# The convolutions' second stage on sixteen 32x32 tiles of TensorE, with another order of channels and the engines' order tied by hand

## The chip, the cores and the metric

The kernel runs on one core of a Trainium2 chip. The metric is the device time of one execution in microseconds (us). The engines are named as in the profile: PE (TensorE's matmuls; PEld its weight loads), DVE (VectorE), ACT (ScalarE), POOL (GpSimd) and SP (SyncE, which here only issues DMAs). PE writes to PSUM, which has eight banks, and reads SBUF.

## What is computed

Four residual layers over x of 2048 rows by 640 channels: attention, convolution, attention, convolution, each behind a layer norm.

```python
x = x + _A_ref(_layernorm(x), A_wqkv, A_wo)      # 32 heads of 20, softmax
x = x + _B_ref(_layernorm(x), ...)
x = x + _A_ref(_layernorm(x), A_wqkv, A_wo)
x = x + _B_ref(_layernorm(x), ...)

def _B_ref(u, log_A_real, A_imag, C_real, C_imag, log_dt, D_skip):
    ...
    K = 2.0 * jnp.einsum("dn,dnl->dl", C, P).real        # a kernel of 2048 taps a channel
    Kf = jnp.fft.rfft(K, L2)                              # L2 = 2 * 2048
    Uf = jnp.fft.rfft(u_t, L2)
    y = jnp.fft.irfft(Uf * Kf[None, :, :], L2)[:, :, :L]
    ...
    return y + u * D_skip[None, None, :]
```

Both convolutions use the same K, so it is made and transformed once.

## The kernel before, in words

Position l of the 2048 is 16 p + i, with p on the 128 partitions and i from 0 to 15. The transforms are written as matmuls in two stages: a first over p (matrix `e1`, 128 frequencies k), a second over i (matrix `f2`, 16 by 16, real and imaginary parts), then the product with the transformed K, and the two stages back (`fa` over i, `eb` over p). Channels go in five blocks of 128 (`NCT`).

**Convolution** (`ssm`). A block has eight steps, 40 in all, n in the code, and some more at the end for the pipeline. Step n of the loop issues:
- `stage2a(n)`: eight f16 transposes of what the first stage left in x1 (the high and the low half of each value), 4 groups of channels, to PSUM `pst`; ACT copies it to `xt`.
- `stage2b(n-1)`: three matmuls of 128 rows by 512 columns with `f2` into `psx`. `f2` is 16 by 16 repeated for the four channels of a group (128 rows: 32 of i and part, 4 channels). Then the product: DVE shuffles psx (real and imaginary parts change places) to t2 and multiplies psx by ka to t1; POOL multiplies t2 by kb and adds the two. ka and kb are loaded from the DRAM tensors `kha`, `khb`.
- `stage1` of the next block: twelve matmuls to PSUM psx1, ACT casts it to x1's high half, DVE subtracts for the low half.
- `stage3(n-3)`: `fa` on the product t1, to `psv`; ACT copies it to v.
- in every second step from n = 11 `stage4`: sixteen rows of records (eight f32 matmuls in two passes) with `eb` to `psy`; DVE adds psy to x, and in the first convolution takes the statistics for the next layer norm (`bn_stats`, four).

In the last block's steps (n from 32) there is no first stage. The last four `stage4` follow the loop. PSUM has the pools X, M, T and F of two banks each: psx1 in X, pst in T, psx in F, psv and psy in M.

**The transform of K** (`ktransform`) does the same two stages with f32 values and no way back: transposes of K by time, first stage, transposes of x1 (`kx`), and one f32 matmul with `f2` for each four groups; DVE writes its result out twice with `stream_shuffle` (real parts doubled, imaginary parts doubled), ACT puts the sign on one, and both go to `kha` and `khb`. It is a generator whose pieces are issued inside the **output projection** of the first attention (`out_proj`, 16 rows s of 30 matmuls `po`). The framework orders instructions by what is ready; where an order is wanted, `tie` makes one instruction follow another on its engine.

The first attention makes K itself (`kgen`) between its exponentials, with an order that a plan sets; `bound` there works out a scale, `ksc`, that the transform uses. `prefetch` loads what the projection needs while the attention ends.

Of the kernel before, what the change touches and what calls it, by code (L numbers as in the profile page):

```python
# [21 lines left out]
P = 128  # L22
# [65 lines left out]
def mha_s4d_kernel(ctx, tc, x_in, wqkv, wo, lar, aim, cr, ci, ldt, dsk,  # L88
                   c_e1, c_eb, c_f2, c_fa, c_sel, c_lv, c_id, c_sg, c_e16, c_f16, c_id16, c_dn, out, parts="asas", general=None):
# [28 lines left out]
    kha = dram.tile([P, D // 4, P], F32, name="kha")  # L118
    khb = dram.tile([P, D // 4, P], F32, name="khb")
# [69 lines left out]
    def chain(ins):  # L189
        last[0] = tie(ins, last[0])  # L190

    def kgen():
# [166 lines left out]
        for n, t in enumerate((ld["cr"], ld["ci"], skip)):  # L359
            ve.reduce_max(big[:, n:n + 1], t, axis=AX.X, apply_absolute_value=True)  # L360
# [12 lines left out]
        slow.append((1, bound))  # L373
        load_powers(2)
        yield
# [771 lines left out]
    def prefetch(x, rest):  # L1147
# [16 lines left out]
        if rest:  # L1164
            with tc.tile_pool(name="wos", bufs=NCT, side="right") as ws:
                for ct in range(NCT):
                    wt = ws.tile([P, D], F32, name="wot")
                    sy.dma_start(wt, wo[ct * P:ct * P + P, :])
                    ge.tensor_copy(woh[:, ct, :], wt)
                    ge.tensor_sub(wol[:, ct, :], wt, woh[:, ct, :])  # L1170
# [20 lines left out]
    ups = []  # L1191
# [16 lines left out]
    SWAP = list(range(16, 32)) + list(range(16))  # L1208
    DUP0 = list(range(16)) * 2
    DUP1 = list(range(16, 32)) * 2  # L1210

    def by_channel(x1, i2):
        return x1[:, :, i2].rearrange("p g (s c) -> p s g c", c=4)

    def ktransform(e1):

        c = ExitStack()
        c1 = c.enter_context(tc.tile_pool(name="f1", bufs=1))
        c2 = c.enter_context(tc.tile_pool(name="f2", bufs=2))
        f2 = c1.tile([P, P], F32, name="f2")  # L1220
        sy.dma_start(f2, c_f2)
        sgn = c1.tile([P, 1], F32, name="sgn")
        sy.dma_start(sgn, c_sg)

        skip = c1.tile([P, NCT], F32, name="skip")
        sy.dma_start(skip, dsk)

        def load(b):
            kl = c2.tile([P, L], F32, name="kl")
            sy.dma_start(kl, kd[b * P:b * P + P, :])  # L1230
            return kl
        kls = [load(0)]

        def unit_load(b):
            kl = kls.pop()
            if b + 1 < NCT:
                kls.append(load(b + 1))
            ve.tensor_add(kl[:, 0:1], kl[:, 0:1], skip[:, b:b + 1])
            hi, lo = (c1.tile([P, NI, P], F16, name=f"ktr{n}") for n in "hl")
            klv = kl.rearrange("d (p i) -> d i p", i=NI)  # L1240
            for i4 in range(4):
                pt = pst("T", [P, 4, P], F32, tag="T", name="pkt")
                for i in range(4):
                    te.transpose(pt[:, i, :], klv[:, 4 * i4 + i, :], ident)
# [3 lines left out]
                yield  # L1248
            x1 = c1.tile([P, 32, NI // 2, 16], F32, name="kx1")
            for i2 in range(NI // 2):  # L1250
                ps = pst("X", [P, 2, 2, P], F32, tag="X", name="pkx")
                for i in range(2):
                    s = 2 * i2 + i
                    for r in range(2):
                        for n, (e, m) in enumerate(((0, hi), (0, lo), (1, hi))):
                            te.matmul(ps[:, r, i, :], e1[:, e, s, r, :], m[:, s, :], start=(n == 0), stop=(n == 2))
                (ve.tensor_copy if i2 % 4 == 1 else se.copy)(by_channel(x1, i2), ps.rearrange("p r i (g c) -> p (r i) g c", c=4))
                yield
            prev = None
            for q in range(9):  # L1260
                if q < 8:
                    pt = pst("T", [P, 4, P], F32, tag="T", name="pkt")
                    for g in range(4):
                        te.transpose(pt[:, g, :], x1[:, 4 * q + g].rearrange("p i s -> p (i s)"), ident)
                    xt = c2.tile([P, 512], F32, name="kxt")
                    se.activation(xt, pt.rearrange("p g k -> p (g k)"), AF.Copy, scale=ksc[:, 1:2])
# [436 lines left out]
```

## Time and profile before

| | us |
|---|---|
| three runs | 2677.0 to 2681.95, median 2681.47 |
| the profiled execution | 2680.85 |
| its span, first to last instruction | 2679.1 |

The mean granted clock of PE was 0.996 over the span. The stages of the profiled execution, in us from the start of the span:

| stage | from | to | length |
|---|---|---|---|
| first attention, with the making of K | 0 | 1102.9 | 1102.9 |
| its output projection, with the transform of K from 1133.5 to 1247.6 | 1102.9 | 1273.6 | 170.7 |
| last layer norms, first stage of the first block | 1273.6 | 1284.85 | 11.25 |
| first convolution | 1284.85 | 1425.1 | 140.25 |
| second attention | 1425.1 | 2470 | 1044.9 |
| its output projection, norms, first stage | 2470 | 2533 | 63 |
| second convolution | 2533 | 2672.5 | 139.5 |

The rows that the prediction quotes are of four kinds. A view by stretches has for each the length and the busy time and number of instructions of PE, PEld, DVE, ACT and POOL, then the granted clock and the DMA engines' share and rate. A view by order of time has start, length, engine, line, operation, what it writes and reads, shape and number of merged instructions, and in brackets the idle time of the engine before it and what ended it. The chain of waits is the work that ended last, followed back. Groups by line have the busy time, the mean in ns and the idle time before them. A busy PE row holds the tail of a matmul that overlaps the next; the pace is read from start to start. Line 78 is a helper through which DVE, ACT and the DMAs are called.

### The profile page before, as it was taken

Reading aid. Unit: us, or ns where it says so; the run is one execution under the profiler, and the core shown is the slowest. Engines: PE = TensorE matmul, PEld = TensorE weight load, DVE = VectorE, ACT = ScalarE, POOL = GpSimd, SP = SyncE. Lnnn points to the kernel's source line nnn. Section 1 sums busy time; section 2 is a strip of 40 time slices with the busy share of each in tenths; the row PEclk is TensorE's granted clock in tenths of the full one; section 3 lists DMA queues with packets and bytes.
Section 4 is the critical chain, followed back from the end, with each engine's and each line's share of the span. In section 5 each row is a group of like instructions: output and inputs, shape, how many; then the busy total and the mean of one; then the engine's idle time right before and its main releaser. Section 6 shows DMA issues by size and latency. Waiting matters only on the chain.

```text
span 2679.1 us, 116332 instructions
## 1 busy us (share of the span) xinstructions
PE 2530.0 (94%) x51106; PEld 1425.0 (53%) x51106; DVE 1516.0 (57%) x3451; ACT 2368.7 (88%) x2793; POOL 827.7 (31%) x1256
## 2 busy tenths in 40 slices
PE   7899999999999998899998999999999998999898
PEld 3445444444444443678896444454444443444788
DVE  8687777886855994477776333232233221154865
ACT  7889999999999999676655799999999999999564
POOL 1123323333323334301672122222222222222376
PEclk9999999999999999999999999999999999999999
DMA  6513222322221224364542121121121113222465
GB/s 210 181 49 86 67 76 55 87 55 76 52 61 49 54 68 155 110 233 162 189 151 69 40 59 50 50 58 47 45 65 38 54 30 93 69 67 60 145 190 162
DMA packets 186580, 242.18 MB, mean 90 GB/s; under 512 B 43376, under 2 KB 128976, under 8 KB 184400
## 3 DMA queue, kind: packets, MB, share of 16 engines
q1 hardware_dynamic: 150048, 188.35, 21.8%
q0 software_dynamic: 36016, 46.30, 7.0%
q8 instruction: 403, 6.60, 1.0%
q14 instruction: 113, 0.93, 0.1%
HBM read 158.50 MB, written 76.01 MB: 88 GB/s over the span
## 4 chain that ended last, share of the span: by engine, by line
ACT 52%; PE 25%; issue 10%; DVE 6%; DMA 3%; POOL 1%; SPq 0%; ACTq 0%; DVEq 0%; POOLq 0%
ACT pt L78 50%; PE pa L892 4%; PE psv L1419 3%; PE psy L1429 3%; PE S L858 3%; PE psx L1407 2%; PE m L611 1%; PE psx L1384 1%; PE po L1312 1%; DMA kop<-ks 1%; PE pst L1394 1%; PE pkf L1272 1%; DVE ktab L78 1%; PE po L1307 1%; PE pq L764 1%
## 5 line engine op out<-in xcount | busy, mean ns | idle before, releaser
L78 ACT ACTIVATE pt<-S 128x1024 f32<-128x1024 f32 x2048 | 1928.6, 1032 | 41.4 <-PE S L858 29.2
L892 PE MATMUL pa<-pt,V 64*32 64x512 f32 x16384 | 1100.9, 590 | 1.4 <-DVE oc L78 1.2
L858 PE MATMUL S<-qop,kop 61*32 61x512 f16 x16384 | 882.9, 381 | 85.2 <-ACT pt L78 68.4
L858 PEld LDWEIGHTS <-kop 61*32 61x32 f16 x16384 | 366.7, 89 | 741.1 <-issue 622.4
L892 PEld LDWEIGHTS pa<-pt,V 64*32 64x32 f32 x16384 | 315.1, 106 | 74.6 <-issue 9.7
L78 POOL DMA_DIRECT2D dn<-oc x252 | 124.5, 501 | 670.6 <-DVE oc L78 643.8
L78 DVE TENSOR_SCALAR qc<-m 128x512 f32<-128x512 f32 (+1 forms) x68 | 46.8, 689 | 303.6 <-PE m L611 303.6
L78 POOL DMA_DIRECT2D db<-dn x252 | 128.0, 514 | 135.1 <-DMA dn<-dr 132.1
L78 DVE COPY oc<-pa 128x512 f32<-128x512 f32 x64 | 44.1, 690 | 199.6 <-PE pa L892 191.9
L611 PE MATMUL m<-xh,wh 64*32 64x512 f16 x2560 | 147.9, 379 | 5.5 <-DVE qc L78 5.5
L78 POOL DMA_DIRECT2D ot<-oc x256 | 130.4, 516 | 71.6 <-DVE oc L78 42.8
L611 PE MATMUL m<-xh,wl 64*32 64x512 f16 x2560 | 148.1, 377 | 0.0
L611 PE MATMUL m<-xl,wh 64*32 64x512 f16 x2560 | 146.7, 376 | 0.0
L611 PEld LDWEIGHTS <-wh 64*32 64x32 f16 x5120 | 92.9, 93 | 78.4 <-issue 36.4
L78 ACT COPY xt<-pst 128x1024 f16<-128x1024 f16 x80 | 81.6, 1022 | 47.2 <-PE pst L1394 47.0
L1412 POOL TENSOR_TENSOR t<-t,kb 128x512 f32<-128x512 f32 x80 | 102.0, 1276 | 67.6 <-DVE t L78 66.7
L78 POOL DMA_DIRECT2D dn<-dr x63 | 35.3, 560 | 248.8 <-DVE dr L78 236.4
L78 DVE TENSOR_SCALAR V<-m 128x160 f32<-128x160 f32 x64 | 20.7, 324 | 158.5 <-PE m L577 158.5
L78 DVE TENSOR_TENSOR kb<-ktab 128x512 f32<-128x512 f32 x160 | 107.7, 692 | 0.0
L577 PEld LDWEIGHTS <-xh 128*128 128x128 f16 x960 | 79.7, 98 | 47.0 <-issue 31.6
L1413 POOL TENSOR_TENSOR t<-t,t 128x512 f32<-128x512 f32 x78 | 99.3, 1273 | 8.5 <-DVE t L78 2.6
L329 PEld LDWEIGHTS m<-kb,ka 128*32 128x32 f32 x3840 | 61.0, 109 | 72.1 <-issue 55.3
(305 smaller groups left out, 4020.7 us busy)
## 6 DMA issues: line engine op xcount, KB each, us to landing
ka<-kha SPq DMA_DIRECT2D x80, 256.0 KB
kb<-khb SPq DMA_DIRECT2D x80, 256.0 KB
db<-dn POOLq DMA_DIRECT2D x252, 64.0 KB, 2.6
kop<-ks SPq DMA_DIRECT2D x176, 80.0 KB
kpw<-wd POOLq DMA_DIRECT2D x60, 192.0 KB, 4.7
qop<-qs SPq DMA_DIRECT2D x256, 40.0 KB
ot<-oc POOLq DMA_DIRECT2D x256, 40.0 KB, 3.0
kha<-kn SPq DMA_DIRECT2D x20, 512.0 KB
```

The costliest lines, as they stand in the source:

```text
L78: made = f(out, *a, **k)
L329: chain(te.matmul(ps[32 * j:32 * j + 32, c8, :], a[n][:, ch, :], b[n][:, dd, :], start=(n == 0), stop=(n == 2), tile_position=(0, 32 * j)))
L577: chain(te.matmul(ps[:, :n], a_[:, ct, sl], m[:, ct, :], start=(k == 0), stop=(k == 14)))
L611: chain(te.matmul(ps[r][32 * t:32 * t + 32, :], a_[rows, ct, 32 * u:32 * u + 32], m[rows, ct, 512 * v:512 * v + 512], start=(k == 0), stop ...
L764: te.matmul(pq, a_[:, ct, :], m[:, ct, sl], start=(n == 0), stop=(n == 14))
L858: chain(te.matmul(S[32 * t:32 * t + 32, 512 * r:512 * r + 512], kt_[rows, kc + 32 * t:kc + 32 * t + 32], qt[rows, :], start=True, stop=Tru ...
L892: chain(te.matmul(pa[r][32 * j:32 * j + 32, :], V[rows, kt, VP * h:VP * h + 32], pts[j // 2][rows, 512 * (j % 2):512 * (j % 2) + 512], sta ...
L1407: te.matmul(px, f2[:, f, :], xt[:, k, :], start=(n == 0), stop=(n == 2))
L1412: ge.tensor_mul(t2, t2, kb)
L1413: (ge if g0 else ve).tensor_add(t1, t1, t2)
L1419: te.matmul(pv[:, g].rearrange("p r i c -> p (r i c)"), t1[:, g * P:g * P + P], fa, start=True, stop=True)
L1429: te.matmul(py[:, i, :], eb[:, 4 * i4 + i, r, :], v[:, r, 4 * i4 + i].rearrange("p g c -> p (g c)"), start=(r == 0), stop=(r == 1))
```

## The change

Channels of a block are grouped 32 apart (c, c+32, c+64, c+96) instead of four neighbours. After the transposes each of the four sits on 32 partitions of its own. The second stage then needs a 32 by 32 matrix for each channel, and four steps are done at once by `sets`: on each of the sixteen tiles of 32 by 32 three matmuls of 512 columns, into four PSUM banks. The transposes read x1 at a distance of 32 elements. The pool T goes; F has four banks for the four channels, and transposes and first stage share X. In the convolutions every engine's order is tied as issued.

```diff
@@ ssm @@
+            def at(name, made):
+                order[name] = tie(made, order.get(name))
...
-            def stage2a(x1, q):
-                pt = pst("T", [P, 2, 4, P], F16, tag="T", name="pst")
+            def stage2a(x1, q, xt):
+                pt = pst("X", [P, 2, 4, P], F16, tag="X", name="pst")
                 for k in range(2):
                     for g in range(4):
-                        te.transpose(pt[:, k, g, :], x1[k][:, 4 * q + g].rearrange("p i s -> p (i s)"), id16)
-                xt = c2.tile([P, 2, 512], F16, name="xt")
-                se.copy(xt, pt.rearrange("p k g c -> p k (g c)"))
-                return xt
+                        at("pe", te.transpose(pt[:, k, g, :], of_group(x1[k], 4 * q + g), id16))
+                at("act", se.copy(xt[:, :, q % 4], pt))
...
-                px = pst("F", [P, 512], F32, tag="F", name="psx")
-                for n, (f, k) in enumerate(((0, 0), (0, 1), (1, 0))):
-                    te.matmul(px, f2[:, f, :], xt[:, k, :], start=(n == 0), stop=(n == 2))
+            def sets(xt):
+                px = [pst("F", [P, 512], F32, tag=f"F{ch}", name=f"psx{ch}") for ch in range(4)]
+                for n, (f, k) in enumerate(((0, 0), (0, 1), (1, 0))):
+                    for ch in range(4):
+                        rows = slice(32 * ch, 32 * ch + 32)
+                        for g in range(4):
+                            mm(px[ch][32 * g:32 * g + 32, :].rearrange("p (q k) -> p q k", k=P), f2[rows, f, :],
+                               xt[rows, k, :, g, :], start=(n == 0), stop=(n == 2), tile_position=(32 * ch, 32 * g))
+                return px
...
+            def product(px, ka, kb, alone):
                 t2 = c2.tile([P, 512], F32, name="t2")
-                ve.stream_shuffle(t2, px, SWAP)
-                ve.tensor_mul(t1, px, ka)
-                ge.tensor_mul(t2, t2, kb)
-                (ge if g0 else ve).tensor_add(t1, t1, t2)
-                return t1
+                at("dve", ve.stream_shuffle(t2, px, SWAP))
+                at("dve", ve.tensor_mul(ka, px, ka))
+                for f, *a in (("tensor_mul", kb, t2, kb), ("tensor_add", ka, ka, kb)):
+                    if alone:
+                        at("dve", getattr(ve, f)(*a))
+                    else:
+                        at("pool", getattr(ge, f)(*a))
+                return ka
...
-            for n in range(NQ + 3 + 4):
+            for n in range(NQ + 9):
                 b, q = divmod(n, 8)
+                if n % 4 == 0 and 4 <= n <= NQ:
+                    px = sets(xt)
                 if n < NQ:
...
-                    xts[n] = stage2a(x1, q)
-                if 1 <= n <= NQ:
-                    t1s[n - 1] = stage2b((n - 1) // 8, (n - 1) % 8, xts.pop(n - 1))
+                    stage2a(x1, q, xt)
+                if 2 <= n < NQ + 2:
+                    ks[n - 2] = factors(*divmod(n - 2, 4))
+                if 4 <= n < NQ + 4:
+                    t1s[n - 4] = product(px[n % 4], *ks.pop(n - 4), n > NQ and n % 2 == 1)
...
-                if 3 <= n < NQ + 3:
+                if 5 <= n < NQ + 5:
...
-                    stage3(vs[bb], qq, t1s.pop(n - 3))
-                if 11 <= n < NQ + 3 and (n - 11) % 2 == 0:
+                    stage3(vs[m // 2], m % 2, ch, t1s.pop(n - 5))
+                if 13 <= n < NQ + 5 and n % 2:
...
@@ ktransform: one group on sixteen tiles, evacuated without shuffles @@
-                    px = pst("F", [P, 512], F32, tag="F", name="pkf")
-                    te.matmul(px, f2, prev, start=True, stop=True)
-                    for s in range(2):
-                        ve.stream_shuffle(kn[s][:, (q - 1) % 2, :], px, [DUP0, DUP1][s])
-                    se.activation(kn[1][:, (q - 1) % 2, :], kn[1][:, (q - 1) % 2, :], AF.Copy, scale=sgn)
+            def ends(t, xt, s, dst):
+                px = [pst("F", [P, 512], F32, tag=f"F{ch}", name=f"pkf{ch}") for ch in range(4)]
+                for ch in range(4):
+                    rows = slice(32 * ch, 32 * ch + 32)
+                    for g in range(4):
+                        matmul(px[ch][32 * g:32 * g + 32, :].rearrange("p (q k) -> p q k", k=P), f2[rows, s, :],
+                               xt[rows, :, g, :], start=True, stop=True, tile_position=(32 * ch, 32 * g))
...
+            steps = [(turned, 0, xts[0], 0), (turned, 0, xts[0], 1), (by_time, b + 1, 0), (ends, 0, xts[0], 0, kha),
+                     (turned, 1, xts[1], 0), (ends, 0, xts[0], 1, khb), (turned, 1, xts[1], 1), (by_time, b + 1, 1),
+                     (ends, 1, xts[1], 0, kha), (first_stage, b + 1, 0), (ends, 1, xts[1], 1, khb),
+                     (first_stage, b + 1, 1), (first_stage, b + 1, 2), (first_stage, b + 1, 3)]
...
@@ out_proj: each matmul of the first projection tied, a step of the transform after every six @@
+            matmul(*a, **k)
+            many[0] += 1
+            if many[0] % 6 == 0:
+                weave(1)
...
-                if s == 2:
-                    weave(1000)
...
@@ kgen @@
-        slow.append((1, bound))
         load_powers(2)
+        slow.append((3, bound))
...
@@ prefetch: the transform's tiles, with K's first block loaded while the attention ends @@
+            rest.extend((small, lambda: load_kl(0)))
...
@@ seq @@
-                psum(c, M=2, T=2, F=2)
+                psum(c, M=2, F=1)
```

`by_time`, `first_stage` and `turned` are the old pieces of the transform, each with two PSUM tiles of X. The sign and the doubling of the transform's results are now in its matrix `c_f2` (one for kha, one for khb). The products of steps 41 and 43 run on DVE alone.

What stands on the engines in the first convolution's loop. DVE, before, from the product t1_29529 to the addition of psy_29667, which is the psy behind that product's psv (psv_29660):

```order
L78 TENSOR_TENSOR t1_29529<-psx_29525,ka_29521 128x512
L78 TENSOR_TENSOR x11_29176<-psx1_29535,x10_29175 128x4x32x4
L78 TENSOR_TENSOR x_25341<-x_25341,psy_29557 128x4x128
L78 BN_STATS st5_28671<-x_25341 128x6 x4
L78 STREAM_SHUFFLE t2_29591<-psx_29586 128x512
L78 TENSOR_TENSOR t1_29590<-psx_29586,ka_29582 128x512
L78 TENSOR_TENSOR x11_29597<-psx1_29598,x10_29596 128x4x32x4
L78 STREAM_SHUFFLE t2_29640<-psx_29635 128x512
L78 TENSOR_TENSOR t1_29639<-psx_29635,ka_29631 128x512
L78 TENSOR_TENSOR x11_29597<-psx1_29645,x10_29596 128x4x32x4
L78 TENSOR_TENSOR x_25341<-x_25341,psy_29667 128x4x128
```

DVE, after, from the addition of one psy to that of the next, psy_30189, behind the psv of the product ka_29967:

```order
L78 TENSOR_TENSOR x_25341<-x_25341,psy_30039 128x4x128
L78 BN_STATS st5_28884<-x_25341 128x6 x4
L78 STREAM_SHUFFLE t2_30120<-psx0_30053 128x512
L78 TENSOR_TENSOR ka_29967<-psx0_30053,ka_29967 128x512
L78 TENSOR_TENSOR x11_29879<-psx1_30125,x10_29878 128x4x4x32
L78 STREAM_SHUFFLE t2_30161<-psx1_30054 128x512
L78 TENSOR_TENSOR ka_30008<-psx1_30054,ka_30008 128x512
L78 TENSOR_TENSOR x11_29879<-psx1_30166,x10_29878 128x4x4x32
L78 TENSOR_TENSOR x_25341<-x_25341,psy_30189 128x4x128
```

The kinds of rows follow each other as before; the product that an odd step's psv takes stood ahead of the previous psy's addition and now stands behind it.

PE, before, at the end of an odd step and the start of the next:

```order
L1384 MATMUL psx1_29645<-uh_26463,e1s_26468 128x128
L1419 MATMUL psv_29660<-fa_26471,t1_29529 128x128 x4
L1429 MATMUL psy_29667<-v_28954,eb_28682 128x128 x8
L1394 LDWEIGHTS x10_29175
L1394 MATMUL pst_29681<-id16_26470,x10_29175 128x128
```

PE, after, the same place ahead of the first rows of a set (48 matmuls of 32 partitions by 512 columns, psx0 to psx3):

```order
L1411 MATMUL psx1_30263<-uh_26471,e1s_26476 128x128
L1411 MATMUL psv_30278<-fa_26479,ka_30116 128x128 x4
L1411 MATMUL psy_30285<-v_29688,eb_28895 128x128 x8
L1411 LDWEIGHTS f2s_26477
L1411 MATMUL psx0_30299<-xt_30105,f2s_26477 32x512
L1411 LDWEIGHTS f2s_26477
L1411 MATMUL psx0_30299<-xt_30105,f2s_26477 32x512
```

psy stands directly behind psv in both; the set comes after psy, once in four steps, in place of three matmuls in each step.

PE at the start of the first output projection, before:

```order
L1307 MATMUL po<-woh,ol 128x320 x10
L1312 MATMUL po<-woh,oh 128x320
L1312 MATMUL po<-wol,oh 128x320
L1312 MATMUL po<-woh,oh 128x320
L1312 MATMUL po<-wol,oh 128x320
```

and after:

```order
L193 MATMUL po<-woh,ol 128x320 x6
L196 MATMUL pkt<-ident,kl 128x128 x8
L193 MATMUL po<-woh,ol 128x320 x4
L193 MATMUL po<-woh,oh 128x320
L193 MATMUL po<-wol,oh 128x320
L196 MATMUL pkt<-ident,kl 128x128 x8
```

The transform's transposes (pkt from kl) now stand among the first row's po, six apart, where before the first row's po stood together.

214 lines of the change are left out of this document (116 added, 98 removed).

## The prediction

> **What bounds the kernel now.** I read the chain of waits first, then the busy time of each engine by stage, then the order of time inside one stage. The chain's shares by engine:
>
> ```profile
> ACT 52%; PE 25%; issue 10%; DVE 6%; DMA 3%; POOL 1%; SPq 0%; ACTq 0%; DVEq 0%; POOLq 0%
> ```
>
> ACT's half is the exponentials of the two attentions, which the change leaves alone. Its stages are the first output projection with the kernels' transform inside it, and the two convolutions. In the view by stretches these are the first three rows (projection alone, with the transform, alone again) and the last two:
>
> ```profile
> 1102.90:1133.50 30.60, 28.44 (x191) 27.09 (x185) 21.96 (x56) 11.78 (x17) 15.68 (x22) 1.00 0.49 152
> 1133.50:1247.60 114.10, 112.90 (x925) 86.59 (x926) 86.65 (x236) 88.70 (x145) 5.64 (x4) 1.00 0.56 213
> 1247.60:1273.60 26.00, 26.00 (x173) 25.04 (x171) 19.57 (x56) 12.71 (x20) 8.26 (x6) 1.00 0.28 100
> ...
> 1284.85:1425.10 140.25, 137.82 (x1434) 123.03 (x1434) 101.88 (x260) 81.66 (x151) 104.79 (x93) 1.00 0.48 155
> ...
> 2533.00:2672.50 139.50, 136.98 (x1407) 121.49 (x1407) 84.90 (x169) 80.38 (x148) 100.02 (x79) 1.00 0.60 188
> ```
>
> PE (first number after the length) is busy nearly throughout all five; POOL comes to 105 of 140 us in a convolution. By shares PE binds and work taken from PE is time won. Whether that holds depends on latency, so here is one pair of steps of the first convolution in order of time (start, length, engine):
>
> ```profile
> 1336.04 1.95 PE L1429 MATMUL psy<-v,eb 128*128 128x128 f32 x16
> ...
> 1337.82 0.61 PE L1394 MATMUL pst<-id,x 128*128 128x128 f16 x8
> 1338.02 0.69 DVE L78 TENSOR_TENSOR x<-x,psy 128x512 f32<-128x512 f32 x1 [1.39 <-PE psy L1429]
> 1338.27 0.81 PE L1407 MATMUL psx<-xt,f2s 128*128 128x512 f16 x3
> ...
> 1338.74 0.87 DVE L78 BATCH_NORM_STATS2 st<-x 128x6 f32<-128x128 f32 x4
> 1338.92 0.22 PE L1384 MATMUL psx<-uh,e1s 128*128 128x128 f16 x1
> ...
> 1339.54 0.73 DVE L78 STREAM_SHUFFLE t<-psx 128x512 f32<-128x512 f32 x1
> 1339.59 1.11 PE L1419 MATMUL psv<-fa,t 128*128 128x128 f32 x8
> 1339.79 0.59 ACT L78 CAST x<-psx 128x512 f16<-128x512 f32 x1 [0.25 <-PE psx L1384]
> ...
> 1340.35 1.27 POOL L1412 TENSOR_TENSOR t<-t,kb 128x512 f32<-128x512 f32 x1 [1.99 <-DVE t L78]
> ...
> 1340.76 0.68 DVE L78 TENSOR_TENSOR x<-psx,x 128x512 f16<-128x512 f32 x1
> ...
> 1341.70 1.28 POOL L1413 TENSOR_TENSOR t<-t,t 128x512 f32<-128x512 f32 x1
> ...
> 1342.30 1.11 PE L1419 MATMUL psv<-fa,t 128*128 128x128 f32 x8
> ...
> 1342.94 1.27 POOL L1412 TENSOR_TENSOR t<-t,kb 128x512 f32<-128x512 f32 x1
> ...
> 1343.24 1.95 PE L1429 MATMUL psy<-v,eb 128*128 128x128 f32 x16
> ```
>
> PE runs without a gap from psy to psy: 7.20 us a pair, of which each step's three psx matmuls take 0.65 (1338.27 to 1338.92). The rows of DVE and POOL are the second thing to see. After psy, DVE adds it to x, takes statistics, shuffles psx; POOL multiplies and adds. That product is finished at 1342.98, 6.94 us after psy began. The psv at 1342.30 doesn't need it: it uses a product that was issued one step earlier.
>
> **The change, part by part.** *The convolutions' second stage.* Three 128-row matmuls in each of four steps (4 x 0.65 = 2.60 us) become one set of 48 matmuls on sixteen tiles. No run shows sixteen tiles; the nearest are eight:
>
> ```profile
> 664.58 0.41 PE L858 MATMUL S<-qop,kop 61*32 61x512 f16 x8
> 664.92 0.54 PE L329 MATMUL m<-kb,ka 128*32 128x64 f32 x24
> 665.40 0.41 PE L858 MATMUL S<-qop,kop 61*32 61x512 f16 x8
> 665.62 1.04 PE L892 MATMUL pa<-pt,V 64*32 64x512 f32 x16
> ```
>
> Eight S matmuls of 512 columns take 0.22 us before the next group starts (665.40 to 665.62), where a single one, a third of the psx rows above, takes 0.22 as well: tiles run beside each other. Where the tiles' shape changes (S to m) the step is 0.34, so a change of shape costs about 0.12. A set is then 3 x 0.22 plus two changes, some 0.95 us, if sixteen behave as eight do; if none ran beside another it would be 48 x 0.22 = 10.6. I take 0.95, the nearest row: 1.65 less PE work in four steps, 16.5 in a convolution.
>
> *The product's place.* The same edit lets the psv of step n take the product issued in step n-1, where it was n-2 (the order's rows above this prediction). DVE's order is kept: x+psy, statistics, then the even step's shuffle. So the odd step's psv, with that step's psy queued behind it on PE, waits for a product that could begin only after the previous odd step's psy. That closes a loop: 6.94 us from psy to the product's end, a hand-over, and 0.94 from psv to psy (1342.30 to 1343.24). The hand-over is 0.06 where PE was already waiting for POOL:
>
> ```profile
> 1412.02 1.27 POOL L1413 TENSOR_TENSOR t<-t,t 128x512 f32<-128x512 f32 x1
> ...
> 1413.35 1.16 PE L1419 MATMUL psv<-fa,t 128*128 128x128 f32 x8 [0.34 <-POOL t L1413]
> ```
>
> A pair cannot be shorter than 6.94 + 0.06 + 0.94 = 7.94 us, whatever PE saves. In the second convolution the statistics are missing, and the shuffle can follow x+psy at 1338.74 instead of 1339.54: 7.14. There are 16 psy ahead of the last four, 15 pairs. Their first and last, in the chain:
>
> ```profile
> 1314.57 1.79 PE psy L1429 x16
> ...
> 1414.51 1.79 PE psy L1429 x16
> ...
> 2562.21 1.79 PE psy L1429 x16
> ...
> 2661.82 1.79 PE psy L1429 x16
> ```
>
> Before, 99.9 and 99.6 us, since the last five pairs, which have no first stage, took less PE time. After: 15 x 7.94 = 119.1 and 15 x 7.14 = 107.1. **Terms +19.2 and +7.5.** The set lies inside the wait and costs nothing there; without the loop it would be on the path. Behind the 16th psy the work is the same.
>
> *The fill.* The first psy stood 29.7 us after the first transpose (row below); it moves from step 11 to step 13. Transposes and first stage now share the two X buffers, so a step cannot be shorter than first stage, cast and subtraction: 0.67 + 0.20 + 0.59 + 0.68 and hand-overs, 2.2. Four steps are 8.5, the set with its latency 1.15, shuffle and hand-over 0.83; then nine products at POOL's pace, 2.59 each (1340.35 to 1342.94), 23.3; hand-over and psv 1.0. That makes 34.8: **+5.2 in each convolution.**
>
> ```profile
> 1284.85 0.62 PE L1394 MATMUL pst<-id,x 128*128 128x128 f16 x8
> ```
>
> *The layout.* The transposes' weights now stand 64 bytes apart in SBUF. Before, only kl's transposes read so (L1244), beside contiguous kx (L1264):
>
> ```profile
> L1264 PE MATMUL pkt<-ident,kx 128*128 128x128 f32 x160 | 23.5, 274 | 0.1
> ...
> L1244 PE MATMUL pkt<-ident,kl 128*128 128x128 f32 x80 | 12.7, 283 | 0.5 <-issue 0.5
> ```
>
> 9 ns of 274: I take nothing, up to 0.45 us a step (eight transposes at double pace) for f16. In the loop that lies in PE's wait; in the fill it would be 2 us a convolution. [...]
>
> *The transform in the projection.* Of PE's work 40 f32 matmuls over 128 rows go, for 20 groups on sixteen tiles:
>
> ```profile
> 1156.15 1.88 PE L1272 MATMUL pkf<-kxt,f 128*128 128x512 f32 x4
> 1157.87 0.83 PE L1244 MATMUL pkt<-ident,kl 128*128 128x128 f32 x6
> ...
> 1248.20 2.92 PE po L1312 x20
> ```
>
> The x4 are two matmuls in two passes each: 0.86 us for one, 34.4 in all. A group costs one such time and two changes of shape and 0.06 for starting sixteen: 1.16, or 23.2. **Term -11.2.** DVE loses 80 shuffles and ACT 40 sign copies, and both take over evacuations:
>
> ```profile
> L78 DVE STREAM_SHUFFLE kn<-pkf 128x512 f32<-128x512 f32 x80 | 54.2, 737 | 0.0
> ...
> L78 ACT ACTIVATE kn<-kn,sgn 128x512 f32<-128x512 f32 x40 | 28.3, 721 | 1.5 <-DVE kn L78 0.9 <-DVE va L78 0.2
> ```
>
> For the 54.2 us DVE gets 40 evacuations, ten more copies and 20 scalings of 512 columns at 0.69 (as x+psy above), 48 us: it stays near 122 of 128 us and is not the bound. PE's order is now fixed by hand, a transform step after every six po, so a step that waits for one of two X buffers stops po too; before, the stage had 3.4 us idle. The bounds: at best PE's bare pace, 480 po at 0.146 (the x20), 480 first-stage matmuls at 0.056 (twelve in 0.67), 240 transposes at 0.11 (the x6) and the groups, 147 us against 170.7, or -24; at worst +5, the waits costing 16. I take -11.2, where the idle stays as it is. The moved scale (bound) and kl's earlier load lie beside ACT's exponentials: nothing; if not, a wait of about a us once.
>
> **Sum**, against the profiled execution's 2680.85 us (span 2679.1; the median of the three runs is 2681.47, 0.6 above): 19.2 + 7.5 + 10.4 - 11.2 = +25.9, so **2707**.
>
> **The rivals.** *PE stays the bound (faster).* If DVE and POOL were through in the time that PE needs from one psy to the next psv, nothing would wait. PE's side is psy 1.78, two transposes, two first stages and one psv, 4.94 us (5.9 with a set); the product's is 7.00. It decides if that falls by 1 to 2 us, say if the shuffle did not stand behind the statistics and POOL's two operations overlapped. Then each convolution gives 16.5 less 5.2, together -22.6, and with the transform -34: 2647. Against it: the rows show no overlap, and DVE's order is printed. *The fixed order costs what it saves (slower still).* The transform at +5 instead of -11.2: 2723. For it: two X buffers hold what T, F and X held, and DVE is three quarters busy. *Loss and gain cancel:* the transform at -24, DVE a little quicker: 2680 to 2690. *The tiles run one after another*, and the change doesn't do what it says: 20 sets at +8 and 20 groups at 16 x 0.86 instead of 1.16 would give over 3000; the S rows speak against it. [...]
>
> **How the numbers follow.** Forecast 0.60, slower still 0.19, PE-bound 0.13, cancelling 0.06 (0.04 of it within 0.2%, about what a measurement of this kernel can tell from no change, 0.02 slower), tiles in turn 0.02. Slower 0.60 + 0.19 + 0.02 + 0.02 = 0.83, same 0.04, faster 0.13. The forecast's own bounds are 13 us down and 16 up from the transform and some 8 either way from fill and hand-overs. The range 2682 to 2738 takes these in with the slower rival and leaves out the two extremes.
>
> **What would show it.** Right: psv in the odd steps idle before it for POOL's addition, pairs of psy near 7.9 and 7.1 us apart, psx sets near 1 us; POOL's share in the convolutions falling below 70%. Wrong: pairs near 6.4, PE without idle time there, or sets of several us. In the projection, po waiting for X buffers would show the second rival. The number is wrong above all if POOL's two operations or DVE's shuffle come sooner after psy than the rows of before allow.

## The result, and the profile after

The changed kernel takes 2738.92 us (median, 2737.35 to 2741.01) beside 2680.74: a ratio of 1.0223, 95% interval 1.0209 to 1.0238. Slower, as forecast, but by 58 us and not by 26. The two profiled executions are 59.2 us apart (2740.04 and 2680.85). The view by stretches of the changed kernel, with the columns explained above, cut at the first and the last po, then for each convolution the fill, the first ten pairs of psy, the next five, and the whole:

```profile
1103.47:1278.47 175.00, 162.03 (x1846) 132.87 (x1841) 121.06 (x257) 91.52 (x151) 28.46 (x32) 0.96 0.51 186
1288.63:1325.60 36.97, 31.70 (x496) 28.34 (x497) 22.35 (x45) 26.18 (x44) 23.70 (x19) 0.95 0.63 219
1325.60:1406.15 80.55, 67.90 (x938) 62.70 (x937) 52.81 (x129) 41.80 (x78) 50.99 (x42) 0.99 0.39 134
1406.15:1452.62 46.47, 31.32 (x306) 29.41 (x305) 24.30 (x59) 12.02 (x26) 21.21 (x17) 0.83 0.28 95
1288.63:1465.19 176.56, 143.02 (x1824) 132.18 (x1824) 106.31 (x264) 81.49 (x153) 101.06 (x90) 0.93 0.39 132
2569.43:2606.34 36.91, 31.76 (x497) 28.30 (x497) 22.36 (x45) 26.13 (x44) 23.68 (x19) 0.96 0.64 218
2606.34:2678.95 72.61, 66.56 (x938) 62.06 (x937) 45.06 (x89) 41.62 (x78) 50.88 (x41) 1.00 0.65 181
2678.95:2719.01 40.06, 28.52 (x306) 26.64 (x305) 20.23 (x39) 12.02 (x26) 21.64 (x18) 0.88 0.53 149
2569.43:2731.56 162.13, 138.93 (x1824) 128.70 (x1824) 90.41 (x176) 81.07 (x152) 96.20 (x76) 0.95 0.58 173
```

The same stretches before are 170.54; 29.56, 72.08, 27.85, 140.26; 29.05, 72.08, 27.53, 139.46. Two things are to be seen. PE, busy for all of the ten pairs before, is now idle for 12.7 of 80.6 us. And the clock column, 1.00 everywhere in these stretches before, is 0.83 and 0.88 in the five pairs of the last block. Against the forecast's terms:

| us | forecast | measured |
|---|---|---|
| fill, each convolution | +5.2 | +7.4, +7.9 |
| ten pairs, first and second convolution | +7.3, -0.7 | +8.5, +0.5 |
| five pairs of the last block | +11.9, +8.2 | +18.6, +12.5 |
| behind the 16th psy | 0 | +1.8, +1.8 |
| projection with transform | -11.2 | +4.5 |
| all else | 0 | -4.2 |
| sum | +25.9 | +59.2 |

One pair of the first convolution after the change, in order of time:

```profile
1365.65 1.95 PE L1411 MATMUL psy<-v,eb 128*128 128x128 f32 x16
...
1367.64 0.69 DVE L78 TENSOR_TENSOR x<-x,psy 128x512 f32<-128x512 f32 x1 [2.35 <-PE psy L1411]
1368.37 0.88 DVE L78 BATCH_NORM_STATS2 st<-x 128x6 f32<-128x128 f32 x4
...
1369.16 0.73 DVE L78 STREAM_SHUFFLE t<-psx 128x512 f32<-128x512 f32 x1
...
1369.97 1.30 POOL L1460 TENSOR_TENSOR kb<-t,kb 128x512 f32<-128x512 f32 x1 [2.79 <-DVE t L78]
...
1371.35 1.27 POOL L1460 TENSOR_TENSOR ka<-ka,kb 128x512 f32<-128x512 f32 x1
...
1372.68 1.16 PE L1411 MATMUL psv<-fa,ka 128*128 128x128 f32 x8 [0.39 <-POOL ka L1460]
...
1373.67 1.95 PE L1411 MATMUL psy<-v,eb 128*128 128x128 f32 x16
```

This is the loop of the forecast, link by link: 6.97 us from psy to the product's end (6.94 forecast), 0.06 to psv, 0.99 to the next psy; 8.02 in all, where 7.94 was forecast. And one pair of the last block:

```profile
1406.15 3.13 PE L1411 MATMUL psy<-v,eb 128*128 128x128 f32 x16
...
1409.32 0.69 DVE L78 TENSOR_TENSOR x<-x,psy 128x512 f32<-128x512 f32 x1 [5.57 <-PE psy L1411]
...
1414.31 1.16 PE L1411 MATMUL psv<-fa,ka 128*128 128x128 f32 x8 [3.08 <-POOL ka L1460]
...
1415.31 3.49 PE L1411 MATMUL psy<-v,eb 128*128 128x128 f32 x16
```

The chain is the same, but psy takes 3.13 us instead of 1.95, and psy is part of the loop. The granted clock was a half from 1405.2 to 1408.6 us, and again from 1415.4 to 1418.9. No forecast term had that. In the projection, the view of waits (engine and what waited, releaser; total, times, longest) has 13.1 us for PE, where before it had 2.7:

```profile
PE pkt L196 <- ACT kxt L78: 4.0, 3, 2.3
PE po L193 <- DVE x L78: 2.2, 1, 2.2
PE pkx L193 <- DMA e1s<-in_c_e: 2.0, 1, 2.0
PE pkx L193 <- ACT kx L78: 1.6, 1, 1.6
PE pkx L193 <- DVE kx L78: 1.4, 1, 1.4
PE pkt L196 <- DVE ktrl L78: 1.1, 2, 0.8
PE pkt L196 <- DVE kxt L78: 0.8, 1, 0.8
...
DVE kl L78 <- DMA kl<-kd: 4.7, 3, 3.1
```

### The profile page after: what moved, and what is told of

Read it like the earlier page. It is cut to its first block, busy times and chain, and to the rows that moved or that the text cites. A ratio compares the mean times of both kernels' runs of the same rounds, so it can differ in the third digit from the quotient of the medians.

```text
span 2738.3 us, 118779 instructions
## 1 busy us (share of the span) xinstructions
PE 2526.4 (92%) x52386; PEld 1431.6 (52%) x52386; DVE 1510.0 (55%) x3367; ACT 2345.3 (86%) x2763; POOL 814.8 (30%) x1250
## 5 line engine op out<-in xcount | busy, mean ns | idle before, releaser
L1460 POOL TENSOR_TENSOR kb<-t,kb 128x512 f32<-128x512 f32 x76 | 96.9, 1275 | 125.7 <-DVE t L78 88.8
L1411 PE MATMUL psv<-fa,ka 128*128 128x128 f32 x640 | 94.5, 293 | 40.2 <-POOL ka L1460 40.1
L78 ACT COPY v<-psv 128x256 f32<-128x256 f32 x160 | 51.8, 376 | 85.0 <-PE psv L1411 83.2
L1411 PEld LDWEIGHTS psv<-fa,ka 128*128 128x128 f32 x640 | 81.5, 199 | 46.6 <-POOL ka L1460 46.0
```

What stands on the lines that cost most here:

```text
L78: made = f(out, *a, **k)
L1411: at("pe", te.matmul(*a, **k))
L1460: at("pool", getattr(ge, f)(*a))
```

## The experiments

The questions: is the pair set by the loop through DVE; does the clock make the last block long; and what took the transform's gain. The first attention, which none of the edits below touches, took between 1103.4 and 1110.2 us up to the first po in the profiles of the changed kernel and of these runs (1102.9 before the change), so stages are compared, and whole times only where they differ by more than that.

**DVE's order alone.**

```diff
+                def rest():
+                    at("dve", ve.tensor_add(x[:, s4, bs], x[:, s4, bs], py))
...
+                return rest
...
                     t1s[n - 4] = product(px[n % 4], *ks.pop(n - 4), n > NQ and n % 2 == 1)
+                if late:
+                    late.pop()()
...
-                    stage4(bb, vs[bb], qq // 2)
+                    late.append(stage4(bb, vs[bb], qq // 2))
```

> The changed kernel with one thing moved in DVE's order: the addition x+psy and the statistics of an odd step stand behind the next step's product (shuffle and multiplication by ka) instead of ahead of it. Loop theory (the pair is set by psy, x+psy, statistics, shuffle, POOL's two operations, psv): the loop is broken, pairs of psy fall from 8.01 and 7.26 us to PE's own work of 6.3 to 6.6 in both convolutions, PE has hardly a gap, the granted clock stays at 1.00 in the last block, and the kernel takes some 2685 to 2695 us. Rival (transposes and first stage share the two X banks, and that sets the pair): pairs stay above 7.5 us, the kernel above 2725. Rival (POOL's pace): pairs stay, POOL without a gap.

Measured 2707.78 us, ratio 1.0098 (1.0081 to 1.0115). Ten and five pairs of both convolutions:

```profile
1330.86:1401.92 71.06, 65.46 (x939) 61.81 (x937) 53.34 (x131) 41.62 (x78) 50.98 (x41) 1.00 0.47 150
1401.92:1433.53 31.61, 26.00 (x307) 24.27 (x305) 20.69 (x56) 12.03 (x26) 21.93 (x18) 0.95 0.46 142
...
2593.26:2662.27 69.01, 65.56 (x938) 61.91 (x937) 45.77 (x92) 41.62 (x78) 51.05 (x41) 1.00 0.67 191
2662.27:2693.60 31.33, 25.98 (x306) 24.25 (x305) 16.69 (x36) 12.03 (x26) 21.66 (x18) 0.95 0.68 190
```

The convolutions fall from 176.6 and 162.1 to 150.5 and 148.1: one move in DVE's order takes back 40 us. Pairs alternate, 6.4 us without a set and 7.95 and 7.4 with one; the expected 6.3 to 6.6 held for the first kind alone, the clock in the last block was 0.95 and not 1.00, and the whole time is 13 us above its band. The rivals (X banks, POOL's pace) fall as what set the pair of 8.0 us: the edit touches neither, and the kernel is well below 2725.

**The old distance, DVE's order untouched.**

```diff
-                if 2 <= n < NQ + 2:
-                    ks[n - 2] = factors(*divmod(n - 2, 4))
+                if 3 <= n < NQ + 3:
+                    ks[n - 3] = factors(*divmod(n - 3, 4))
...
-                    stage3(vs[m // 2], m % 2, ch, t1s.pop(n - 5))
+                    stage3(vs[m // 2], m % 2, ch, t1s.pop(n - 6))
...
-                if 13 <= n < NQ + 5 and n % 2:
+                if 14 <= n < NQ + 6 and n % 2 == 0:
```

> The changed kernel with the old distance given back: the psv of a step takes the product issued two steps earlier, as before the change, so that everything from psv on comes one step later; the factors are loaded one step later too, so that four buffers do; DVE's order is not touched. Loop theory: pairs fall from 8.01 and 7.26 us to 6.4 to 7.4 in both convolutions as with DVE's order moved, though the fill gets 2.6 to 3.3 us longer, and the last block runs at full clock. Rival (the gain of the moved addition came from the first stage's banks being freed earlier, not from the product): pairs stay at 8.

Measured 2706.52 us, ratio 1.0097 (1.0077 to 1.0117).

```profile
1332.62:1403.95 71.33, 65.46 (x926) 61.13 (x925) 51.12 (x125) 40.94 (x78) 49.15 (x40) 1.00 0.45 147
1403.95:1432.89 28.94, 24.43 (x299) 22.33 (x298) 22.05 (x59) 11.39 (x26) 22.33 (x18) 1.00 0.52 163
...
2590.82:2656.57 65.75, 64.26 (x926) 61.20 (x925) 43.84 (x87) 41.10 (x78) 49.66 (x40) 1.00 0.69 193
```

Either end of the loop can be opened: with two steps between product and psv the ten pairs come to 71.3 and 65.8 us, and the last block runs at full clock. So the one step that the change took away is what made the pairs long, not the tiles. It is not the whole loss: the convolutions take 150.9 and 145.4 us, 10.7 and 5.9 more than before the change, and the fill alone 8.7 and 8.8 more.

**More work in the last block.**

```diff
-                if n < NQ and b + 1 < NCT:
+                if n < NQ:
...
-                    low = stage1(b + 1, nxt, q)
+                    low = stage1(min(b + 1, NCT - 1), nxt, q)
```

> The changed kernel with work added: in the last block, where no first stage is left, a first stage is done once more, and its result is used by nobody (12 matmuls, a cast and a subtraction in each of eight steps). Clock theory (PE waits over 3 us at a stretch there, its granted clock falls to a half, and psy then takes 3.1 to 3.6 us instead of 1.95, inside the loop): with the added work the clock stays at 1.00, psy stays at 1.95, pairs of the last block fall from 8.3 to 10.2 us to about 8.0 in the first convolution and from 7.1 to 8.9 to about 7.3 in the second, and the kernel gets some 8 to 15 us faster although it does more. Rival (the products that run on DVE alone, or the factors' loads, lengthen the last pairs): pairs stay as they are or get longer, and the kernel takes 2737 to 2750 us.

```profile
1412.65:1452.99 40.34, 29.28 (x378) 27.04 (x377) 28.31 (x65) 15.48 (x32) 21.64 (x18) 0.99 0.37 112
...
2680.90:2718.32 37.42, 30.01 (x378) 27.95 (x377) 24.66 (x46) 15.41 (x32) 21.91 (x18) 0.95 0.55 158
```

With 96 matmuls more, the five pairs of the first convolution take 40.34 us at clock 0.99: 8.0 a pair, the loop's own length. How much that gains has to be read beside the four runs on the projection below, which leave the convolutions as they are in the changed kernel. There the same five pairs took 43.2 to 45.5 us at clocks of 0.85 to 0.92, and 37.6 at 0.95 in the second convolution. One of the four:

```profile
1409.87:1453.11 43.24, 27.83 (x307) 25.91 (x305) 24.30 (x59) 12.03 (x26) 21.59 (x18) 0.92 0.33 104
...
2684.37:2721.92 37.55, 25.97 (x307) 23.96 (x305) 19.98 (x39) 12.03 (x26) 21.63 (x18) 0.95 0.57 160
```

So the changed kernel's own profile, 46.47 and 40.06, is the longest of five, and the added work gains 2.9 to 6.1 us in the first convolution; in the second its 37.42 us are no gain that can be told from 37.6. The clock's part is shown in the first convolution alone: the lower the clock, the longer the five pairs, from 40.34 at 0.99 to 46.47 at 0.83. The whole time, 2739.69 us, did not fall by the expected 8 to 15 us: the first attention took 5.8 us longer in this profile than in the changed kernel's.

**More work for PE alone.**

```diff
+                elif n < NQ:
+                    ps = pst("X", [P, 2, 2, P], F32, tag="X", name="psx1")
+                    for k in range(24):
+                        mm(ps[:, 0, 0, :], e1[:, 0, 0, 0, :], uh[:, 0, :P], start=True, stop=True)
```

> The changed kernel with 24 more matmuls of 128 by 128 in each of the last block's eight steps, into a bank that nobody reads; ACT, DVE and POOL get nothing more. They are 1.3 us of PE work a step at full clock, laid into the wait that stands there. Clock theory: PE's longest wait falls below 2 us, the clock stays at 1.00 up to step 40, and the first six pairs of the last block fall from 8.4 to 9.5 us to 8.0 in the first convolution and to 7.1 to 7.5 in the second: the convolutions get some 5 to 7 and 2 to 4 us shorter with 192 matmuls more in each. Rival (the last block's pairs are long for want of something that ACT, DVE or POOL deliver): they stay, or get longer by the added 2.7 us.

```profile
1324.36:1408.10 83.74, 73.09 (x987) 68.01 (x985) 52.77 (x129) 41.89 (x78) 50.87 (x42) 0.96 0.40 128
1408.10:1450.07 41.97, 33.89 (x451) 32.19 (x449) 24.18 (x59) 12.25 (x26) 21.39 (x17) 0.96 0.34 107
...
2679.73:2718.80 39.07, 33.40 (x450) 32.05 (x449) 19.94 (x39) 12.25 (x26) 20.76 (x17) 0.96 0.51 150
```

Half a success at most. The five pairs take 41.97 us in the first convolution, at 0.96, beside 43.2 to 46.5 without the added work; in the second 39.07 us are longer than the 37.6 of four such runs, since pairs with a set, where PE had no room, rise to 8.4. And the granted clock of the first convolution's ten pairs was 0.96, and they rose to 83.74; the run that wove the transform later, without any edit here, had ten pairs of 83.35 us at 0.96 as well, where the changed kernel's own took 80.55 at 0.99. So how long a convolution runs at half clock differs from profile to profile, without an edit there. Whole time 2742.26 us (ratio 1.0230, 1.0213 to 1.0247): no gain.

**The projection: order, start, and one DVE instruction.** Four runs. The changed kernel's stage took 175.0 us in its own profile and 173.2 to 177.6 in five runs whose edits leave it alone, so a difference of 2 us says nothing here. First, po not tied, the transform in one piece behind the third row:

```diff
-            if filler[0] is None:
...
-            matmul(*a, **k)
-            many[0] += 1
-            if many[0] % 6 == 0:
-                weave(1)
+            te.matmul(*a, **k)
...
+                if s == 2:
+                    weave(1000)
```

> The changed kernel with the first output projection's matmuls not tied, and the transform issued in one piece behind the third row as before the change; the transform itself keeps its sixteen tiles. Theory that the fixed order costs what the tiles save: the stage of projection and transform falls from 175 to about 160 us (170.7 less 11), and the kernel to some 2722 to 2728. Rival (the tiles' groups, or evacuations on DVE and ACT, bound the stage): 170 to 178 us, the kernel at 2733 or more.

Measured: the stage took 181.43 us, the kernel 2750.71 (ratio 1.0262, 1.0242 to 1.0283). Taking the fixed order away alone does not bring the gain back. The waits of DVE and PE there name another cause:

```profile
DVE kl L78 <- DMA kl<-kd: 12.3, 4, 5.0
...
PE pkx L193 <- DVE kx L78: 10.0, 4, 3.9
```

K's next block is loaded into one buffer now (two before), and DVE's one-column addition to it stands early in DVE's order: DVE waits for the load with all evacuations behind it. Second, weaving from the third row on (`many[0] > 60`):

> The changed kernel with the transform's steps woven in from the third row on (after 60 po matmuls) instead of from the first. If the stage's loss comes from its start, where PE waits 2 us for the load of e1s and then runs 3.4 us at half clock, the stage falls by 4 to 6 us to about 170; if it comes from the waits further on (DVE for the load of kl, ACT's norms ahead of kxt), it stays within 2 us of 175.

174.25 us, with one group of the transform (1.35 us) left behind the last po, and 2741.8 for the kernel: the start is not it. Third and fourth, the addition tied behind the evacuation of the step before its own, in the changed kernel and in the untied one:

```diff
-                ve.tensor_add(kl[:, 0:1], kl[:, 0:1], skip[:, b:b + 1])
+                tie(ve.tensor_add(kl[:, 0:1], kl[:, 0:1], skip[:, b:b + 1]), behind[0] and behind[0].ins)
...
-                        ve.tensor_scalar_mul(xt[:, q], pt, ksc[:, 1:2])
+                        behind[0] = ve.tensor_scalar_mul(xt[:, q], pt, ksc[:, 1:2])
```

> The changed kernel with one instruction tied in the transform: DVE's addition of the skip to K's next block (kl), which stood early in DVE's order and waited up to 3.1 us for the block's load with the projection's additions queued behind it, now follows the evacuation of the step before its own. If this wait makes PE's longest stop in the projection and the half clock behind it (2.2 us for x, 6.8 us at half clock), DVE's wait for kl disappears, and the stage of 175 us falls by 4 to 7 us. If the stage is held by ACT's and DVE's evacuations through two X banks, another wait takes its place and the stage stays within 2 us of 175.

> The same tie for the addition to kl, on top of the projection whose own matmuls are not tied (its stage took 181.4 us with the addition early, DVE waiting 12.3 us for kl). If that wait was what made it longer, the stage falls by 8 to 14 us, to 167 to 173 us. If not, it stays above 178.

```profile
1108.09:1281.47 173.38, 158.97 (x1846) 131.37 (x1841) 120.86 (x257) 91.36 (x151) 28.50 (x32) 0.97 0.52 188
...
1107.24:1278.54 171.30, 163.97 (x1846) 133.60 (x1840) 119.46 (x255) 91.27 (x151) 29.51 (x32) 0.99 0.53 190
```

Tied, DVE's wait for kl is gone and the stage, at 173.38 us, stays within what the unedited one takes, the expectation's second case: other waits take its place (PE waits 3.9 us for ACT's kxt and 3.1 for its kx). Untied, it gains 10.1, to 171.3 us with the clock at 0.99, about the 170.5 of before. So the early addition to kl was what made the untied stage longer. With it out of the way the stage takes 173.4 us in the fixed order and 170.9 to 172.9 in the three untied runs that have the tie (two of them follow below): what the order itself costs is hardly more than the spread, and neither brings the forecast gain. The whole times are 2741.98 and 2738.54 us.

**The set ahead of psy.** On top of the first run; x+psy and the statistics also go behind the first stage's subtraction:

```diff
-                if n % 4 == 0 and 4 <= n <= NQ:
-                    px = sets(xt)
...
+                if n % 4 == 3 and n < NQ:
+                    px = sets(xt)
```

> The kernel with x+psy and the statistics later (which took 150.5 and 148.1 us for the convolutions, pairs of psy 6.4 without a set and 7.95 and 7.4 with one), with two more moves: the set stands between psv and psy instead of behind psy, and x+psy and the statistics stand behind the first stage's subtraction. If pairs with a set are long because DVE's shuffle waits for a set that waits for psy, and the next first stage waits for DVE, they fall to PE's own work of 7.2 to 7.4 us, pairs without stay at 6.4, and the convolutions come to 145 to 148 us each. If the set itself is dear on PE, they stay at 7.4 to 7.95.

Measured 2698.34 us, ratio 1.0072 (1.0056 to 1.0089), convolutions 149.0 and 142.6. In the second, pairs with a set fell to 7.35, as expected, and the other kind rose to 6.5; in the first they came to 8.24 and 6.55, no shorter than before this move, and the convolution missed its 145 to 148. There the next step's shuffle still stands behind the statistics, which is the likely cause and was not tested alone. Inconclusive on the set's own cost; 0.85 us on PE is all that the rows of order of time show for it.

**All remedies together, and two more.** Two steps between product and psv, x+psy behind the next step's subtraction, the projection untied with kl tied:

> Three remedies together: psv two steps behind its product (as in the run of that name), x+psy and the statistics behind the following step's product and subtraction, and the projection's matmuls not tied, with the addition to kl tied. If the two loops through DVE's order were the whole of the convolutions' loss in the middle, pairs come to PE's own work, 6.4 to 7.0 us in both, so a convolution takes fill 38, ten pairs 67, five pairs 27 and the end 11, together 141 to 146 us, and the projection 171; the kernel 2684 to 2692. If another limit stands behind them (POOL's pace of 2.6 a product, ACT's order), pairs stay at 7.1 to 7.8 as with two steps alone, and the kernel at 2692 to 2700.

Measured 2697.13 us, ratio 1.0057 (1.0041 to 1.0074), above the band of 2684 to 2692. The first convolution is 142.7 us, with pairs of 6.4 and 7.0, PE idle for 0.8 of 64.65 us. The second is 149.5, because of DVE's waits for the factor ka and of what stands on SP's queue:

```profile
DVE ka L78 <- DMA ka<-kha: 19.9, 12, 3.5
...
2630.64 0.39 SPq L78 DMA_DIRECT2D out<-x  x1
2631.12 0.46 SPq L78 DMA_DIRECT2D ka<-kha  x1
2631.67 0.40 SPq L78 DMA_DIRECT2D kb<-khb  x1
```

The store of x waits for x+psy, now later, and the loads are queued behind it. The same kernel with the transform's first stage, and a fill's first four transposes, in the sets' four banks:

> The same, with the X banks relieved: the transform's first stage writes to the four banks of the sixteen tiles, and in a convolution's first four steps the transposes do. If X's two banks make the waits of the projection's stage and the length of a fill step (2.2 us), the stage falls from 171 to 163 to 168 us and a fill from 38 to 35 to 36: the kernel gets 8 to 12 us shorter than its neighbour. If ACT's layer norms and evacuations make the waits, the stage stays within 2 us of 171, and the four banks may lengthen it.

Measured 2702.18 us, ratio 1.0070 (1.0053 to 1.0088): the fills gain 1.2 and 1.9 us, but the projection's stage takes 181.7, with PE waiting 8.0 us for DVE to empty those banks (kn). The wait moved from one pool to the other. Last, the three remedies with the fill's first four transposes in the sets' banks again (not the transform's first stage), the stores behind the loads, and the first stage put off in a fill:

```diff
-                        at("sp", sy.dma_start(ov[:, s4, bs], x[:, s4, bs]))
+                        stores.append(lambda: at("sp", sy.dma_start(ov[:, s4, bs], x[:, s4, bs])))
...
+            AT = {2: [0], 3: [1], 4: [2, 3], 5: [4, 5], 6: [6], 7: [7]}
...
-                    low = stage1(b + 1, nxt, q)
+                    for k, i2 in enumerate([q] if b else AT.get(q, [])):
+                        stage1(b + 1, nxt, i2, k and q < 6)()
```

> The three remedies together (2697 us; convolutions 142.7 and 149.5) with two more. First, the second convolution's stores of x stand behind the next step's loads of ka and kb on SP, not ahead of them: if the second convolution was the longer one because SP waited for x+psy with the factors' loads queued behind it (DVE waited 30.9 us for ka), its pairs fall from 7.1 to 8.6 us to 6.4 to 7.0 and its 16 psy from 101 to about 94 us; if DMA bandwidth makes the waits, they stay. Second, in the first four steps the transposes go to the tiles' four banks and the next block's first stage is put off into steps 2 to 7: if a fill step is long because transposes, first stage, cast and subtraction take turns on two banks and ACT (2.2 us a step), the fill falls from 38 us to 33.5 to 35.5 in both; if POOL's nine products set it, to no less than 37. Together some 2678 to 2686 us, beside 2680.5 before the change.

```profile
1289.68:1324.12 34.44, 31.95 (x517) 29.56 (x517) 23.99 (x48) 27.21 (x46) 23.84 (x19) 0.95 0.73 232
1324.12:1388.87 64.75, 63.91 (x926) 61.01 (x925) 50.84 (x129) 40.77 (x78) 51.05 (x42) 1.00 0.52 163
...
2534.18:2569.06 34.88, 32.81 (x516) 30.26 (x517) 23.95 (x48) 27.32 (x46) 24.55 (x20) 0.92 0.67 226
2569.06:2633.64 64.58, 63.79 (x926) 60.89 (x925) 42.64 (x87) 40.77 (x78) 50.00 (x40) 1.00 0.67 198
```

Both held: fills of 34.4 and 34.9, ten pairs of 64.8 and 64.6. The convolutions take 137.8 and 139.1 us, 2.5 and 0.4 less than before the change. The kernel takes 2681.85 us, ratio 1.0005 (0.9996 to 1.0014): with all remedies the change comes to no difference.

## Why the prediction was wrong

**Right: the loop.** "A pair cannot be shorter than 6.94 + 0.06 + 0.94 = 7.94 us, whatever PE saves": it was 8.01 in the first convolution's middle, and 7.14 was 7.26 in the second. Opening the loop at either end gave most of the time back. PE's saving in the second stage, without value inside the loop, is real: with the loop open ten pairs take 64.6 us instead of 72.1, where five sets were to save 8.25.

**Wrong: the loop's length in the last block.** The step that failed multiplied one pair by fifteen. It put the same 6.94 us, with psy at full clock, into every pair. In the last block, where there is no first stage to fill it, PE's wait for the product grew to as much as 3.9 us, the granted clock was a half in several stretches (0.83 and 0.88 over the five pairs), and psy, which is in the loop, took 3.1 to 3.5 us in four of the first convolution's five pairs and 2.8 and 3.5 in two of the second's. That cost 6.7 and 4.3 us beyond the forecast in this profile. How many psy are hit differs from profile to profile: in the four runs that leave the convolutions alone the cost was 3.5 to 5.8 us in the first and 1.9 in the second. With the clock kept up by more work, 15 pairs of the first convolution took 120.5 us, and 119.1 had been forecast; for the second no run shows it. The 1.8 us behind the 16th psy belong here too: the granted clock was a half (0.50) over both 16th psy, which took 3.62 us each, and in two of the four runs the end of the second convolution took 10.8 us as before the change, in the other two 12.4. The forecast read the clock of before (1.00 in every row) as given, though it had itself put waits on PE.

**Wrong: "I take -11.2, where the idle stays as it is".** PE's saving was there. In 16 of the 20 groups 1.07 us pass from a group's first row to the next po, and the first row starts 0.24 behind the last po, where po follow each other at 0.146: together the 1.16 that was taken. No run shows the 0.06 in it for starting sixteen by itself; the rows show the group as a whole. These rows of order of time show one group:

```profile
1129.33 0.31 PE L193 MATMUL po<-wol,oh 128*128 128x320 f32 x1
1129.57 1.14 PE L193 MATMUL pkf<-kxt,f 32*32 32x512 f32 x32
1130.64 1.15 PE L193 MATMUL po<-woh,ol 128*128 128x320 f32 x6
```

PE's busy time in the stage fell by 5.2 us (167.18 to 162.03). The clock was a half in three stretches (from 1111.65, 1176.51 and 1207.23 us), 13.7 us in all. Half of that, 6.8 us, is an estimate of what they added to PE's busy time; at full clock it would have fallen by 12. But the idle did not stay: it rose by 9.6 us, from 3.4 to 13.0, and 9.6 - 5.2 gives the measured +4.5 within rounding. So the waits and the clock, which the term had put at nothing, took more than the whole gain. The slower rival (2723) named the place and put its cause on the order by hand; the untied runs show that this is a small part at most: untied it is longer still, until DVE's wait for kl is taken out, and then some 2 us shorter. What holds the stage at 171 us then, some 12 us above the forecast of 159.3, was not isolated and stays open; PE is idle for 7.3 us there, the rows name evacuations on ACT and DVE, and more banks for one part moved the wait to another.

**Half right: the fill.** Steps of 2.2 us and POOL's pace of 2.59 were right; 2.2 and 2.7 us came on top. At each set POOL's next two products start 3.0 and 2.8 us apart and not 2.59, and the four steps took 9.4 and 9.3 us and not 8.5, the first of them 2.5. The layout cost next to nothing, as taken: eight strided transposes mostly take 0.64 to 0.73 us, 0.67 in the middle, beside 0.61 before, so 0.06 more and not the 0.45 a step that the prediction allowed at most.

The range ended at 2738. Its upper end allowed for one bad stage; the clock had a part in both the projection and the last block, and a common cause is what a range built from separate terms leaves out.

## What to carry to other kernels

Before a gain is booked on a busy engine, close the loops: an edit that shortens the distance between producer and consumer by one step can turn a busy engine into a waiting one (here PE, idle for 12.7 of 80.6 us in the ten pairs). In an order written by hand, a short instruction that waits can hold up what stands behind it on its queue: here DVE's addition to kl waited up to 3.1 us for its load, and with the stores of x ahead of the loads DVE waited 19.9 us for ka, with the stores behind them 1.6. And where a forecast makes PE wait, its clock has to be forecast too: at 0.83 over the five pairs, psy inside the loop went from 1.95 us to as much as 3.5. A profile is one draw of where the half-clock stretches fall (the same five pairs took 43.2 to 46.5 us in five profiles): run a kernel with the stage unedited several times before a gain of a few us is booked.

## What the runs showed of the hardware

Sixteen tiles of 32 by 32 ran beside each other here: 48 matmuls of 512 columns took 0.85 us from the set's start to the next transposes (1367.53 to 1368.38). psy to set is 0.09 us longer than psy to transposes (1365.65 to 1367.53 beside 1373.67 to 1375.46), so a set costs 0.94 us where 0.95 was taken.

The granted clock fell to a half while PE was still partly at work. In the changed kernel's profile the half-clock stretches between 1100 and 1475 us last 3.41 us or twice that, and begin on one grid of 3.41 us. Worked out from the matmuls' rows there, the ten stretches of that grid that came before a fall had PE busy for 14 to 44%, and of those at full clock that were followed by full clock none had less than 49%. In other runs the busy share does not tell the two apart. In the ten pairs of the first convolution PE was busy for 67.73 of 80.41 us at clock 1.00 with the projection untied, and for 70.74 of 83.35 at 0.96 where the transform was woven in later. And in the untied projection with kl tied, the clock was 0.92 from 1139 to 1160 us, with PE busy for 20.27 of these 21 us. What makes it fall was not isolated.
